# The first loads of a four-layer linear-attention and gated-MLP kernel: two x blocks whole, one on each DMA queue, the first weights split over both queues, twelve idle matmuls

## Chip, cores, metric

One core of a Trainium2 chip. The metric is the device time of one execution in microseconds. The profiler takes one execution; the other times have no profile. A profiled execution's own time is its span plus about 1.8 us, so one can say for each profile whether it was a quick or a slow execution of its kernel.

In the lines of the profile, PE is TensorE's matmuls, PEld its loads of the stationary operand, DVE is VectorE, ACT ScalarE, POOL GpSimd and SP SyncE. An idle matmul multiplies zeros and nobody uses its result; it only keeps TensorE busy until data arrives. "Warm" means that matmuls with 512 columns start 0.216 us apart, "cold" that they start 0.43 us apart, at half the clock.

## The reference

Four layers on x of shape (1, 2048, 1024) in bf16, attention and MLP in turn, each with a layernorm ahead and a residual:

```python
x = x + _A_ref(_layernorm(x), A_wqkv, A_wo)      # linear attention, 32 heads
x = x + _B_ref(_layernorm(x), W_gate, W_up, W_down)   # relu-gated MLP, F = 3584
x = x + _A_ref(_layernorm(x), A_wqkv, A_wo)
x = x + _B_ref(_layernorm(x), W_gate, W_up, W_down)

# in _A_ref:
qkv = (x @ wqkv)...
pq, pk = phi(q), phi(k)
kv = einsum("bhsd,bhse->bhde", pk, v)
```

The change touches only what happens in the first 20 us: layernorm of the first four blocks of 128 tokens (x0 to x3), their transposes, and the first units of k = x @ wqkv. "Unit (j, c)" below is block j times the 512 columns kc, 8 matmuls.

## The kernel before

The loads of the head, in program order. A load without a queue goes out from SyncE (SP); `nc.scalar` sends it from ScalarE (ACT). `k0(0, H)` loads the first half of the first weights (4 of 8 tiles of 128 rows, 512 KB), `k1()` loads 1 MB.

```python
for _ in range(10):
    nc.tensor.matmul(idle, lhsT=zero[:, 0:P], rhs=zero, start=True, stop=True)

k0, k1, v0, q0, q1 = (ring.place() for _ in range(5))
self.load_x(0, 0, nc.scalar)      # columns 0..511 of block 0, 128 KB
self.load_x(0, 1)                 # columns 512..1023
self.load_x(1, None, nc.scalar)   # block 1 whole, 256 KB
k0(0, H)
self.load_x(2, None, nc.scalar)
k0(H, 2 * H)
self.load_x(3, None, nc.scalar)
k1()
q0()
self.load_x(4)
# ... cut: x5 to x7, q1, x8 to x15, v0
```

The work that waits for them. VectorE and ScalarE keep this order (a manual schedule):

```python
def block0():
    stat(0, 0); stat(0, 1)     # VectorE, statistics of both halves of x0
    rstd(0)
    stat(1, 0)                 # VectorE, first half of x1: ahead of the scale of x0
    scale(0, 0); scale(0, 1)
    t0 = turn(0, 0); t1 = turn(0, 1)   # 8 transposes on TensorE
    t0("s")
    stat(1, 1); rstd(1)
    t1("v")
    k(0, 0, between)           # 8 matmuls; "between" puts x1's scale and transposes into it
```

Of the kernel before, what the change touches and what calls it, by code (L numbers as in the profile page):

```python
# [18 lines left out]
class _Ring:  # L19
# [9 lines left out]
    def place(self):  # L29

        name, src = self.plan[self.loaded]
        t = self.pool.tile([P, 8, NW], BF16, tag="w")
        self.tiles[name] = t
        self.loaded += 1
        return lambda lo=0, hi=8: self.nc.sync.dma_start(out=t[:, lo:hi, :], in_=src[:, lo:hi, :])

    def load_to(self, n):
        while self.loaded < min(n, len(self.plan)):
# [40 lines left out]
class _Net:  # L79
# [131 lines left out]
    def head(self):  # L211

        nc, tc, ring = self.nc, self.tc, self.ring
        H = self.KT // 2

        zero = self.ep.tile([P, NW], BF16, tag="e")
        nc.vector.memset(zero, 0.0)
        idle = self.ps3.tile([P, NW], F32, tag="b")
        for _ in range(10):
            nc.tensor.matmul(idle, lhsT=zero[:, 0:P], rhs=zero, start=True, stop=True)  # L220

        k0, k1, v0, q0, q1 = (ring.place() for _ in range(5))
        self.load_x(0, 0, nc.scalar)
        self.load_x(0, 1)
        self.load_x(1, None, nc.scalar)
        k0(0, H)
        self.load_x(2, None, nc.scalar)
        k0(H, 2 * H)
        self.load_x(3, None, nc.scalar)
        k1()  # L230
        q0()
        self.load_x(4)
        self.load_x(5)
        self.load_x(6)
        self.load_x(7)
        q1()
        for t in range(8, self.ST):
            self.load_x(t)
        v0()
        src = self.xb  # L240
        self.xnT[0, 0] = self.xnTp.tile([P, self.KT, QT * P], BF16, tag="xnT", name="xnT0_0")
        stats = [self.small.tile([P, 2, nc.vector.BN_STATS_DIM], F32, tag="stats", name=f"st{j}")
                 for j in range(QT)]
        rs, xn = {}, {}

        def stat(j, c):
            self.ln_stat(j, src[j], c, stats[j])

        def rstd(j):
            rs[j] = self.ln_rstd(stats[j])  # L250
            xn[j] = self.xn_home(0, j)

        def scale(j, h=None):
            self.ln_scale(src[j], *rs[j], xn[j], h)

        def turn(j, h):
            tp = self.ps3.tile([P, H, P], BF16, tag="b")
            for i in range(H):
                kt = h * H + i
                nc.tensor.transpose(tp[:, i, :], xn[j][:, kt * P:(kt + 1) * P], self.ident)  # L260
            dst = self.xnT[0, 0][:, h * H:(h + 1) * H, j * P:(j + 1) * P]

            def take(engine):
                if engine == "v":
                    nc.vector.tensor_copy(out=dst, in_=tp)
                else:
                    nc.scalar.activation(out=dst, in_=tp, func=ACT.Copy)

            return take

        return stat, rstd, scale, turn
# [468 lines left out]
```

## Time and profile before

| | before |
|---|---|
| timed runs beside the change | 1629.17, 1629.21, 1629.38, 1629.8 us |
| the execution that was profiled | 1630.68 us (span 1628.9) |
| TensorE busy | 1621.7 us of 1628.9 |
| x0 complete / second half of k0 / k1 | 3.75 / 10.19 / 13.37 us from the start |
| first transposes / first projection matmul / unit (1,0) | 6.38 / 7.46 / 11.56 us |

The completion times are those of the last of the 16 DMA engines that share a transfer.

### The profile page before, as it was taken

Reading aid. Unit: us, or ns where it says so; the run is one execution under the profiler, and the core shown is the slowest. Engines: PE = TensorE matmul, PEld = TensorE weight load, DVE = VectorE, ACT = ScalarE, POOL = GpSimd, SP = SyncE. Lnnn points to the kernel's source line nnn. Section 1 sums busy time; section 2 is a strip of 40 time slices with the busy share of each in tenths; the row PEclk is TensorE's granted clock in tenths of the full one; section 3 lists DMA queues with packets and bytes.
Section 4 is the critical chain, followed back from the end, with each engine's and each line's share of the span. In section 5 each row is a group of like instructions: output and inputs, shape, how many; then the busy total and the mean of one; then the engine's idle time right before and its main releaser. Section 6 shows DMA issues by size and latency. Waiting matters only on the chain.

```text
span 1628.9 us, 18772 instructions
## 1 busy us (share of the span) xinstructions
PE 1621.7 (100%) x7754; PEld 739.3 (45%) x7754; DVE 566.7 (35%) x940; ACT 331.8 (20%) x638; POOL 201.9 (12%) x134
## 2 busy tenths in 40 slices
PE   8999999999999999999999999999999999999999
PEld 4444444444444444444444444444444444444444
DVE  7845695213212222212165547942022111111211
ACT  5741212101110110111066312121011101101110
POOL 2349220000000000000023592100000000000000
DMA  7312647448445444544560147464554454454452
GB/s 245 65 52 56 178 71 206 144 148 232 155 143 190 160 151 161 168 147 137 168 128 1 53 93 250 85 193 146 182 165 152 155 184 155 145 166 154 155 162 71
DMA packets 298246, 235.06 MB, mean 144 GB/s; under 512 B 101296, under 2 KB 294192, under 8 KB 298160
## 3 DMA queue, kind: packets, MB, share of 16 engines
q1 hardware_dynamic: 292832, 228.75, 47.7%
q10 hardware_dynamic: 5328, 5.11, 0.9%
q8 instruction: 60, 0.98, 0.3%
q14 instruction: 26, 0.21, 0.0%
HBM read 201.33 MB, written 8.39 MB: 129 GB/s over the span
## 4 chain that ended last, share of the span: by engine, by line
PE 98%; ACT 1%; DVE 1%; DMA 1%; issue 0%; SPq 0%; DVEq 0%
PE pu L639 24%; PE pg L639 24%; PE acc L663 23%; PE ps L404 12%; PE ps L530 7%; PE ps L439 7%; DMA t<-in_A_wqkv_dram 1%; PE kv L452 0%; PE acc_last L663 0%; ACT e L351 0%; ACT e L350 0%; PE fold L515 0%; DVE st L138 0%; ACT e L352 0%; DVE slab L358 0%
## 5 line engine op out<-in xcount | busy, mean ns | idle before, releaser
L639 PEld LDWEIGHTS <-t 128*128 128x128 bf16 x3584 | 350.3, 98 | 423.2
L639 PE MATMUL pu<-xnT,t 128*128 128x512 bf16 x1792 | 423.5, 379 | 0.0
L639 PE MATMUL pg<-xnT,t 128*128 128x512 bf16 x1792 | 423.4, 379 | 0.0
L663 PE MATMUL acc<-t,hT 128*128 128x512 bf16 x1764 | 382.5, 379 | 0.0
L645 DVE TENSOR_TENSOR hT<-pu,rg 128x512 bf16<-128x512 f32 x224 | 154.7, 691 | 572.0 <-PE pu L639 572.0
L644 ACT ACTIVATE rg<-pg 128x512 f32<-128x512 f32 x224 | 133.5, 596 | 737.3 <-PE pg L639 737.0
L663 PEld LDWEIGHTS <-hT 128*128 128x128 bf16 x1820 | 177.9, 98 | 209.1
L404 PE MATMUL ps<-t,xnT 128*128 128x512 bf16 x1024 | 224.3, 380 | 2.2 <-DMA t<-in_A_wqkv_dram 1.7
L404 PEld LDWEIGHTS <-xnT 128*128 128x128 bf16 x1024 | 99.2, 98 | 122.3 <-issue 4.3
L530 PE MATMUL ps<-T,pqT 128*128 128x512 bf16 x512 | 111.2, 379 | 0.0
L145 ACT ACTIVATE rstd<-mv,eps 128x1 f32<-128x1 f32 x64 | 18.7, 293 | 334.1 <-DVE mv L143 333.9
L680 DVE TENSOR_TENSOR xo<-x,acc 128x512 bf16<-128x512 f32 x31 | 21.3, 688 | 170.3 <-PE acc L663 170.3
L483 POOL TENSOR_TENSOR prod<-pq,zrow 128x1024 f32<-128x1024 bf16 x32 | 67.9, 2122 | 85.9 <-DVE den L488 72.5
L138 DVE BATCH_NORM_STATS2 stats<-x 128x6 f32<-128x512 f32 (+1 forms) x120 | 78.0, 673 | 0.8
L530 PEld LDWEIGHTS <-pqT 128*128 128x128 bf16 x512 | 49.9, 98 | 60.4 <-issue 0.5
L419 POOL CAST ksum<-x 128x512 f32<-128x512 bf16 x2 | 1.7, 866 | 605.4 <-DVE x L358 605.4
L677 DVE TENSOR_TENSOR x<-x,acc 128x512 f32<-128x512 f32 x32 | 21.6, 675 | 138.5 <-PE acc L663 137.4
L421 POOL TENSOR_TENSOR ksum<-ksum,slab 128x512 f32<-128x512 f32 x46 | 54.0, 1183 | 84.6 <-DVE slab L358 75.1
L358 DVE SCALAR_TENSOR_TENSOR pq<-ps,e 128x512 bf16<-128x512 f32 x64 | 44.0, 688 | 53.9 <-ACT e L352 52.2
L495 POOL TENSOR_TENSOR pq<-pq,den 128x1024 bf16<-128x1024 bf16 x32 | 61.7, 1933 | 3.1 <-DVE den L490 3.1
L488 DVE TENSOR_REDUCE den<-prod 128x32 f32<-128x1024 f32 x32 | 39.0, 1217 | 53.9 <-POOL prod L483 53.9
L439 PE MATMUL ps<-slab,x 128*128 128x512 bf16 x256 | 56.6, 379 | 0.0
(57 smaller groups left out, 596.0 us busy)
## 6 DMA issues: line engine op xcount, KB each, us to landing
t<-in_B_W_gate_dram SPq DMA_DIRECT2D x56, 1024.0 KB, 7.1
t<-in_B_W_up_dram SPq DMA_DIRECT2D x56, 1024.0 KB, 5.4
t<-in_B_W_down_dram SPq DMA_DIRECT2D x64, 896.0 KB, 5.2
t<-in_A_wqkv_dram SPq DMA_DIRECT2D x11, 1024.0 KB, 5.6
t<-in_A_wo_dram SPq DMA_DIRECT2D x4, 1024.0 KB, 7.2
away<-x SPq DMA_DIRECT2D x8, 512.0 KB, 4.4
x<-away SPq DMA_DIRECT2D x8, 512.0 KB, 8.5
out_dram<-xo ACTq DMA_DIRECT2D x31, 128.0 KB, 2.5
```

Of the source, the lines that this page charges most:

```text
L138: self.nc.vector.bn_stats(out=stats[:, c, :], in_=src[:, c * fmax:(c + 1) * fmax])
L358: nc.vector.scalar_tensor_tensor(out=out, in0=ps, scalar=0.0, in1=e, op0=ALU.max, op1=ALU.add)
L404: nc.tensor.matmul(by_row(ps), lhsT=self.xnT[l, l_q][:, kt, j * P:(j + 1) * P], rhs=w[:, kt, :].rearrange("p (b i d) -> p i b d", i=R, d=H ...
L421: nc.gpsimd.tensor_tensor(out=ksum[:, cols], in0=ksum[:, cols], in1=pk, op=ALU.add)
L439: nc.tensor.matmul(ps, lhsT=self.xn[l, t][:, d * P:(d + 1) * P], rhs=self.pk[l, t][:, h * NW:(h + 1) * NW], start=(t == 0), stop=(t == sel ...
L483: nc.gpsimd.tensor_tensor(out=prod, in0=pq_of[sc, j], in1=zrow, op=ALU.mult)
L495: nc.gpsimd.tensor_tensor(out=heads(pq), in0=heads(pq), in1=den[:, :].unsqueeze(2).to_broadcast([P, D // HD, HD]), op=ALU.mult)
L530: nc.tensor.matmul(ps, lhsT=pqT[sc][:, g, j * P:(j + 1) * P], rhs=T[g // 2][:, g % 2, n2 * NW:(n2 + 1) * NW], start=(g == 0), stop=(g == G ...
L639: nc.tensor.matmul(ps, lhsT=w[:, kt, fi * P:(fi + 1) * P], rhs=self.xnT[l, q][:, kt, :], start=(kt == 0), stop=(kt == KT - 1))
L644: nc.scalar.activation(out=rg, in_=pg, func=ACT.Relu)
L645: nc.vector.tensor_tensor(out=h[:, fi, :], in0=pu, in1=rg, op=ALU.mult)
L663: nc.tensor.matmul(ps[:, 0:n], lhsT=hT[ft // 4][:, ft % 4, j * P:(j + 1) * P], rhs=wd[:, k, i * n:(i + 1) * n], start=(ft == 0), stop=(ft ...
```

## The change

The intent, as the diff shows it: have the first two blocks arrive together, bring the second half of k0 sooner by giving half of the first weights to each queue, and let x2 and x3 come later; two more idle matmuls so that TensorE stays warm.

```diff
-        for _ in range(10):
+        for _ in range(12):
...
-        self.load_x(0, 0, nc.scalar)
-        self.load_x(0, 1)
-        self.load_x(1, None, nc.scalar)
+        act = nc.scalar
+        self.load_x(0, None, act)
+        self.load_x(1)
+        k0(H, 2 * H, act)
         k0(0, H)
-        self.load_x(2, None, nc.scalar)
-        k0(H, 2 * H)
-        self.load_x(3, None, nc.scalar)
+        self.load_x(2, None, act)
         k1()
+        self.load_x(3, None, act)
         q0()
```

(The helper that places weights got a `queue` argument; its line is cut. Line numbers of the changed kernel are one higher than before.)

More of the change, by code (lines that the diff above doesn't have):

```diff
@@ L34, in place @@
         self.loaded += 1
-        return lambda lo=0, hi=8: self.nc.sync.dma_start(out=t[:, lo:hi, :], in_=src[:, lo:hi, :])
+        return lambda lo=0, hi=8, queue=None: (queue or self.nc.sync).dma_start(
+            out=t[:, lo:hi, :], in_=src[:, lo:hi, :])
     def load_to(self, n):
```

## The prediction

> **What bounds the kernel now.** I began with the page: how full TensorE is, and what the chain that ended last is made of.
>
> ```profile
> span 1628.9 us, 18772 instructions
> ...
> PE 1621.7 (100%) x7754; PEld 739.3 (45%) x7754; DVE 566.7 (35%) x940; ACT 331.8 (20%) x638; POOL 201.9 (12%) x134
> ...
> PE 98%; ACT 1%; DVE 1%; DMA 1%; issue 0%; SPq 0%; DVEq 0%
> ```
>
> TensorE is idle for 1628.9 - 1621.7 = 7.2 us in the whole span. The diff touches only the loads and idle matmuls of the first microseconds, so no part of it can be worth more than a piece of those 7.2 us (0.4%). Asked from 45 us to the end, the waits of TensorE are an empty list: whatever the start gains or loses is handed to the end one for one. The waits of TensorE in the first 20 us are these (us in total, times, longest):
>
> ```profile
> PE ps L404 <- DMA t<-in_A_wqkv_dram: 1.7, 1, 1.7
> PE idle L220 <- DVE zero L217: 1.3, 1, 1.3
> PE tp L260 <- DVE x L154: 0.6, 1, 0.6
> PE ps L404 <- ACT xnT L267: 0.4, 1, 0.4
> ```
>
> The 1.3 us before the first instruction is not touched. The other waits belong to the change. The timeline of the head says in what order they come (start, duration, engine, line, work, and in brackets the idle time before it and its releaser):
>
> ```profile
> 1.34 4.45 PE L220 MATMUL idle<-zero 128*128 128x512 bf16 x10 [1.34 <-DVE zero L217]
> ...
> 3.78 1.29 DVE L138 BATCH_NORM_STATS2 st<-x 128x6 f32<-128x512 bf16 x2 [2.49 <-DMA x<-in_A_x_dram]
> ...
> 6.38 0.72 PE L260 MATMUL tp<-ident,x 128*128 128x128 bf16 x8 [0.58 <-DVE x L154]
> ...
> 7.46 1.04 PE L404 MATMUL ps<-t,xnT 128*128 128x512 bf16 x4 [0.37 <-ACT xnT L267]
> ...
> 10.23 0.59 PE L404 MATMUL ps<-t,xnT 128*128 128x512 bf16 x2 [1.73 <-DMA t<-in_A_wqkv_dram]
> ...
> 11.56 3.74 PE L404 MATMUL ps<-t,xnT 128*128 128x512 bf16 x16
> ...
> 13.41 1.39 PEld L404 LDWEIGHTS <-xnT 128*128 128x128 bf16 x7 [0.23 <-issue]
> ...
> 19.28 0.45 PEld L260 LDWEIGHTS <-x 128*128 128x128 bf16 x8 [0.57 <-DVE x L154]
> ...
> 19.74 25.48 PE L404 MATMUL ps<-t,xnT 128*128 128x512 bf16 x116
> ```
>
> Four matmuls use the first half of k0, then TensorE stops until 10.23 us for the second half. Two smaller stops follow. The one at 13.41 us is hidden in "x16": sixteen matmuls at the warm pitch would take 15 x 0.216 + 0.38 = 3.62 us, which is what the next such group takes; this group took 3.74 us, so 0.12 us is lost, at the ninth matmul, the first that uses k1. The third, at 19.28 us, is for the scaled fourth block of x: about 0.25 us by the pitch. After 19.74 us there is none.
>
> When do the weights land? The DMA view of narrow windows gives issue to landing of single transfers:
>
> ```profile
> t<-in_A_wqkv_dram SPq DMA_DIRECT2D x1, 512.0 KB, 8.5
> ...
> t<-in_A_wqkv_dram SPq DMA_DIRECT2D x1, 1024.0 KB, 11.2
> ```
>
> The first is the second half of k0, issued at 1.66 us: 1.66 + 8.5 = 10.2 us, the end of the long stop. The second is k1, issued at 2.20 us: 2.20 + 11.2 = 13.4 us, the end of the short one. By the same view the first half of k0 lands at 1.19 + 4.5 = 5.7, x0's halves at 3.5 and 3.8, x1 at 1.19 + 4.0 = 5.2.
>
> **What the Trainium skill says.** "DMA: Bandwidth & Descriptors", section "Issuing engines are not separate DMA queues": transfers started by different engines run on the same 16 DMA engines and interleave. The trace agrees: from 2 to 5 us, with both queues at work, 334 GB/s flow; from 10 to 13.4 us, with almost only SP's queue, 351 GB/s. So a second queue changes who is served first, not how much arrives. The same page, "Queues, rings and completion order": each DMA engine round-robins between the queues that have work. The trace fits that: from 6 to 7 us the two queues take 45% and 51% of the engines' time. "TensorE: Matmul & The Clock Gate", "Part 1: The HAM clock gate": about 3.4 us of sustained work release the full clock, and back-to-back 512-column matmuls are 427 ns apart cold and 216 ns warm. The trace shows both: the idle matmuls come about 0.43 us apart ((4.45 - 0.63) / 9, with 0.63 us for one), the later ones 0.216.
>
> **The change part by part.**
>
> *x0 whole on ACT, x1 whole on SP.* Before, x0 came as two halves of 128 KB side by side. Now 512 KB share the engines before either is complete. At the 385 GB/s that the trace moves from 3 to 4 us, the additional 256 KB take 0.7 us, but before, a part of k0 already rode beside x0's halves, so less is new: counting the bytes moved, 512 KB are through at about 3.7 us, and the landing signal came 0.4 us or so after the data of the small transfers; so 4.1 to 4.2 us instead of 3.75. Cost: +0.4 us on statistics, scale, transposes and the first real matmul, 7.46 to 7.86 us. x1 comes earlier (5.2 to about 4.2), which is of no use: the statistics of x1 start at 5.22 us because VectorE is then free.
>
> *Half of k0 on each queue, directly behind.* Ahead of a complete k0 there are now 0.5 MB of x and 1 MB of k0, instead of also x2, x3 and some of k1. 1.57 MB at 350 GB/s are 4.5 us, from 2.25 to about 6.7, landing at about 7.1 us if all 16 engines keep pace, and up to 2 us later if one lags (the third rival). The matmuls that use the second half are due at 7.86 + 4 x 0.216 = 8.72 us instead of 10.23. From there to the next unit's start the work is the same: 11.56 - 10.23 = 1.33 us. So unit (1,0) starts at about 10.05 instead of 11.56: 1.5 us sooner at this place. That is the 1.9 us by which the fifth matmul was late (10.23 against 7.46 + 4 x 0.216 = 8.32), less the 0.4 us above.
>
> *k1 behind them.* What has to arrive up to the end of k1 is unchanged: four blocks of x, k0 and k1, 3.15 MB, on engines that are already full. So k1 still lands at about 13.4 us if everything else is equal, while TensorE now wants it at 10.05 + 8 x 0.216 = 11.8. TensorE takes its units in order, so most of the 1.5 us can be given back in a new wait in front of k1. At 350 GB/s the 3.15 MB need 9.0 us, to 11.3, with the landing 11.7. The measured 13.4 is therefore not the mean rate alone; the last of the 16 engines came late. If the new order avoids that, k1 costs nothing; if not, it takes nearly all. I put k1's landing at 12.7, between the two: 0.7 us of gain pass it.
>
> *The third stop.* VectorE reaches the second and third norm sooner, by up to 1.5 us, even while TensorE waits for k1, since these depend on x2, x3 and the early copies. So the scale at 19.28 us should no longer be waited for: 0.1 to 0.25 us.
>
> *Two more idle matmuls.* 2 x 0.43 us, ending at 5.79 + 0.86 = 6.65 instead of 5.79 us. The first transposes are now due at 6.38 + 0.4 = 6.78. They fit in the gap: cost 0, and the clock stays released.
>
> Sum: +0.4 for x0, -1.9 for k0's second half, +0.8 given back at k1, -0.2 at the third stop: -0.9 us, less 0.1 for what I cannot see. 1629.4 - 0.8 = 1628.6 us.
>
> **Rivals.**
> 1. *k1 takes the place of k0 in full.* For it: the byte count. Against it: the count alone gives 11.7, not 13.4. It makes 1629.1 to 1629.4.
> 2. *The wait for k0 just vanishes and k1 is in time.* Then 1.5 + 0.2 us are gained: 1627.7. For it: the bytes would fit; against it: the landing of 13.4 in the kernel before.
> 3. *The halves of k0 are themselves caught by a late engine.* The second half of k0 landed at 10.2 although the total rate would have had it sooner; from 5 to 6 us the transfers fell to 302 GB/s. If a DMA engine falls behind by 2 us again, k0 is complete at about 9, unit (1,0) starts near 11, and k1 caps the rest: 1629.0.
> 4. *ACT is held up by issuing.* It now issues a 512 KB transfer between the x blocks. Its four issues took 1.97 us together before; SP's took up to 4.6 us when its queue was full. ACT's first activation is due at 5.7 us; should its last issue block behind SP's, the norm is late by a microsecond or two: 1630 to 1631. ACT queues only 1.25 MB, less than SP had in hand without blocking (2.1 MB), so I give it one chance in ten.
>
> **Range and chances.** Rivals 1 and 3 on one side and 2 on the other span 1627.7 to 1629.4; run to run the kernel varied from 1629.17 to 1629.8, so I add some tenths: 1627.6 to 1630.0. Two per cent would be 32.6 us, more than four times all the idle time of TensorE; within 2% is all but certain.
>
> **What would show it.** In the timeline of after: first statistics near 4.2 us; transposes near 6.8; the first eight projection matmuls with no wait over 0.3 us for k0; unit (1,0) near 10; a wait for k1 between 10 and 13.4 us, of 0 to 1.6 us, 0.9 at my estimate; the run of 116 matmuls starting near 18.9 instead of 19.74. I am wrong if TensorE stops for k0 for over a microsecond, if k1 is no wait at all, if ACT's first activation comes after 6.5 us, or if anything after 45 us changes by more than 0.3 us.

## The result, and the profile after

| | before | after |
|---|---|---|
| median (range) of 4 runs each | 1629.30 (1629.17 to 1629.80) | 1631.86 (1630.82 to 1632.28) |
| profiled execution | 1630.68 | 1632.28 |
| x0 / second half of k0 / k1 complete | 3.75 / 10.19 / 13.37 | 5.23 / 8.95 / 12.57 |
| transposes / first projection / unit (1,0) / run of matmuls without a stop | 6.38 / 7.46 / 11.56 / 19.74 | 7.86 / 8.94 / 12.73 / 20.93 |

The ratio is 1.0014, 95% interval 0.9997 to 1.0032: within 2% without doubt, but above the predicted range (1627.6 to 1630.0). A ratio here is the mean time of one kernel's fast runs over that of the other's of the same rounds, so not quite the ratio of the medians. Over all nine runs of the changed kernel (with e1 below) and 45 of the kernel before, the medians are 1630.84 and 1629.40: about 1.4 us longer instead of a microsecond shorter. The interval of the ratio contains 1; that the change costs time rests on the groups of runs and on the profiles. The profiled execution of the changed kernel is the slowest of its four.

The page of the changed kernel: TensorE is busy for 1623.5 us, 1.8 more than before, and there is a row PEclk that the page of the kernel before has not. Averaged over slices of 41 us it reads 9 everywhere, which looks harmless; the granted clock of the execution is given as 0.999, before as 1.0.

```profile
span 1630.5 us, 18776 instructions
...
PE 1623.5 (100%) x7756; PEld 740.8 (45%) x7756; DVE 566.7 (35%) x940; ACT 331.8 (20%) x638; POOL 202.0 (12%) x134
...
PEclk9999999999999999999999999999999999999999
```

TensorE's waits of the changed kernel (us in total, times, longest). The wait for weights is gone; the wait before the transposes grew from 0.6 to 1.8 us:

```profile
PE tp L261 <- DVE x L155: 1.8, 1, 1.8
PE idle L221 <- DVE zero L218: 1.3, 1, 1.3
PE ps L405 <- ACT xnT L268: 0.4, 1, 0.4
```

The timeline of the changed kernel for the same stretch:

```profile
1.34 4.75 PE L221 MATMUL idle<-zero 128*128 128x512 bf16 x12 [1.34 <-DVE zero L218]
...
5.25 1.29 DVE L139 BATCH_NORM_STATS2 st<-x 128x6 f32<-128x512 bf16 x2 [3.97 <-DMA x<-in_A_x_dram]
...
7.86 0.72 PE L261 MATMUL tp<-ident,x 128*128 128x128 bf16 x8 [1.76 <-DVE x L155]
...
8.94 2.74 PE L405 MATMUL ps<-t,xnT 128*128 128x512 bf16 x6 [0.37 <-ACT xnT L268]
...
12.73 3.62 PE L405 MATMUL ps<-t,xnT 128*128 128x512 bf16 x16
...
20.47 0.45 PEld L261 LDWEIGHTS <-x 128*128 128x128 bf16 x8 [0.57 <-DVE x L155]
```

Three readings. The statistics start at 5.25 us instead of 3.78, and everything up to the first projection matmul is later by the same 1.5 us. Then six matmuls take 2.74 us: (2.74 - 0.63) / 5 = 0.42 us apart, twice the 0.216 of before, and no wait is in them. That is TensorE at half clock, and no list of waits shows it. The view of narrow windows does, in the column of the granted clock (0.50, the third number from the end); in the trace's record the clock is halved from 8.82 to 12.24 us:

```profile
9.00:10.00 1.00, 1.00 (x3) 0.37 (x4) 0.69 (x3) 0.49 (x2) 0.00 (x0) 0.50 1.06 367
```

And the sixteen matmuls from 12.73 us on take 3.62 us, so there is no wait for k1: it landed at 12.57 us, and its unit was due only at 14.46.

A fourth reading stands at the other end of the trace. The last work of VectorE, before (above) and after (below):

```profile
1625.97 0.42 DVE L680 TENSOR_TENSOR xo<-x,acc_last 128x256 bf16<-128x256 f32 x1 [0.34 <-PE acc_last L663]
1627.17 0.42 DVE L681 TENSOR_TENSOR xo<-x,acc_last 128x256 bf16<-128x256 f32 x1 [0.34 <-PE acc_last L664]
```

Up to there the changed kernel is 1.20 us late, but its span is 1.60 us longer (1630.50 against 1628.90). The other 0.40 us come after the last output has landed: from that landing to the end of the span 0.91 us pass before and 1.31 us after, most of the difference being SyncE standing still for 0.37 us (0.06 before) between two of its closing waits, the second for a DMA that had landed 27 us earlier. All six profiles of the changed kernel and of its variants e1, e3, e7, e8 and e15 have this (1.28 to 1.31 us), the other eleven do not (0.84 to 0.99). So it belongs to the program and not to the execution; why, no run shows.

### The profile page after: what moved, and what is told of

Read it like the earlier page. It is cut to its first block, busy times and chain, and to the rows that moved or that the text cites. A ratio compares the mean times of both kernels' runs of the same rounds, so it can differ in the third digit from the quotient of the medians.

```text
span 1630.5 us, 18776 instructions
## 1 busy us (share of the span) xinstructions
PE 1623.5 (100%) x7756; PEld 740.8 (45%) x7756; DVE 566.7 (35%) x940; ACT 331.8 (20%) x638; POOL 202.0 (12%) x134
## 4 chain that ended last, share of the span: by engine, by line
PE 98%; ACT 1%; DVE 1%; DMA 0%; issue 0%; DVEq 0%
PE pu L640 24%; PE pg L640 24%; PE acc L664 23%; PE ps L405 12%; PE ps L531 7%; PE ps L440 7%; PE kv L453 0%; PE acc_last L664 0%; DMA x<-in_A_x_dram 0%; ACT e L352 0%; ACT e L351 0%; DVE st L139 0%; PE fold L516 0%; ACT e L353 0%; DVE slab L359 0%
```

## Experiments

"Before" in the same rounds had nine runs in each set. Pooled, the kernel before has 45 timed runs, 1629.11 to 1630.96 us, in two groups: 26 of them at 1629.44 or less, the other 19 at 1629.78 or more. Its median is 1629.40, its mean 1629.79. Differences of some tenths of a microsecond are therefore told only where the groups of runs do not overlap, or where a profile shows the step.

The theories, as formed after the first comparison: A, the order of the loads makes x0 late in every run; B, one of the 16 DMA engines falls behind by chance, and it was bad luck; C, the longer idle time lets the clock drop, and that is a second cost on top.

### Repeats: the changed kernel (e1) and the kernel before (e2)

No edit.

> The changed kernel once more, nothing edited. Theory A (order): whole blocks of x side by side make x0 land about 1.4 us later, whatever the run; then x0 lands again at 5.0 to 5.4 us and TensorE again idles 1.5 us or more before the first transposes. Theory B (luck of the start): one or some DMA engines stall at the start and it is chance on which transfer it falls; then x0 lands anywhere from 4.1 to 5.4 us. Theory C (clock), which can hold with either: the idle time before the transposes lets the TensorE clock fall to half, seen as matmuls 0.43 us apart after 8.9 us; expected again where the idle time is over 1.5 us. Time 1631 to 1632.3 if A and C.

> The kernel before once more, nothing edited, as the yardstick. A: x0's halves land again at 3.5 to 3.8 us. B: in one of several runs they land a microsecond later. k1's landing tells how steady the late DMA engine is: 13.4 us again if it belongs to the order, 11.7 to 13.4 if it is chance. Ratio to the kernel before 1.000 within 0.0003.

e1: median 1630.18 (1630.02 to 1632.38); in the profile x0 complete at 5.42 us, and the projection matmuls cold again, here from the fourth on. Its median missed the expected 1631 to 1632.3; only the profiled execution is in that range. e2: median 1630.45 (1629.29 to 1630.89); x0's halves at 3.40 and 3.58, k1 at 12.95, between the 11.7 and 13.4 that the expectation called chance. The changed kernel's nine runs of both sets lie between 1630.02 and 1632.38, and its quickest is slower than 30 of the 45 runs of the kernel before. A and C hold so far. e2's ratio is at the edge of 1.000 within 0.0003 (1.0003, with an interval from 0.9990 to 1.0016): the kernel before has two groups of times that I had not known.

### Only the idle matmuls on the kernel before: 12 (e4), 4 (e11)

```diff
-        for _ in range(10):
+        for _ in range(12):      # e4;  range(4) in e11
```

> The kernel before with 12 idle matmuls instead of 10, only this part of the change. They end at about 6.2 to 6.6 us, the transposes are due at 6.38: cost 0 to 0.25 us at the transposes, and none of it later, because the first matmul of the second half of k0 waits for its weights until 10.2 us anyway. Time as before within 0.2 us under every theory; if it is over a microsecond slower, the idle matmuls themselves are the cause.

> The kernel before with 4 idle matmuls instead of 10, loads untouched: the cost of a cold clock alone. C: TensorE idles 3.3 us before the transposes, the first projection matmuls are 0.43 us apart, and the median rises by 0.6 to 1.6 us, to 1630 to 1631. If the clock costs nothing here, as before: 1629.2 to 1629.6.

e4: median 1629.63 (1629.19 to 1630.18), as before. Its profile is worth more than its time: it is a quick execution (1629.19 us), and shows what the kernel before looks like when it is quick. Its timeline:

```profile
6.36 0.72 PE L260 MATMUL tp<-ident,x 128*128 128x128 bf16 x8 [0.18 <-DVE x L154]
7.44 1.04 PE L404 MATMUL ps<-t,xnT 128*128 128x512 bf16 x4 [0.37 <-ACT xnT L267]
8.72 0.59 PE L404 MATMUL ps<-t,xnT 128*128 128x512 bf16 x2 [0.24 <-DMA t<-in_A_wqkv_dram]
```

The stop for the second half of k0, 1.73 us in the profile that I predicted from, is 0.24 us here, with the same loads. The second half of k0 was complete at 8.68 us instead of 10.19. The difference is the last of the 16 DMA engines: k1 landed on the first engine at 11.2 to 11.3 us in both, and on the last 2.04 us after that in the first profile, 0.48 in this one (1.82 in e2, a slow execution of 1630.45 us). So part of B is right, though not of the change: in these three profiles the wait that the change was to remove is long in the two slow executions (1.73 and 1.48 us) and short in the quick one.

e11: median 1631.16 (1630.49 to 1632.07), a little over the expected 1630 to 1631; its five runs overlap with the slowest of before. Its timeline shows the cold clock with the loads untouched, four matmuls (1.89 - 0.63) / 3 = 0.42 us apart:

```profile
6.33 1.03 PE L260 MATMUL tp<-ident,x 128*128 128x128 bf16 x8 [3.10 <-DVE x L154]
7.63 1.89 PE L404 MATMUL ps<-t,xnT 128*128 128x512 bf16 x4 [0.26 <-ACT xnT L267]
```

### The changed kernel with 20 idle matmuls (e3, e15) and with 10 (e7)

```diff
-        for _ in range(12):
+        for _ in range(20):      # e3 and e15;  range(10) in e7
```

> The changed kernel with 20 idle matmuls instead of 12: eight more at 0.216 us once warm fill 1.73 us, up to about 7.8 us, when the transposes of x0 are due. C: the first projection matmuls are 0.216 us apart, the cold stretch is gone, and the kernel is 1.5 to 1.8 us faster than the changed kernel and about 0.5 us faster than the kernel before (k0 and k1 came 0.8 to 1.2 us earlier): 1628.7 to 1629.2 us. If the clock is not the cause (the lateness of x0 alone costs the time): as the changed kernel, 1631 to 1632.

> The changed kernel with 20 idle matmuls once more, for the clock: its x0 landed early (4.54 us) in the first profile, so the cover was hardly tested. C: no run over 1631.5 (nine runs with 12 idle matmuls had four over 1631.6), and in the profile no projection matmuls 0.43 us apart even if x0 lands at 5.2 us or later. If the clock is not the cause of the slow runs, some of these five are over 1631.6 too.

> The changed kernel with 10 idle matmuls as before. They end about 0.4 to 0.8 us sooner, so the idle time before the transposes is 2 us or more. C (clock): the matmuls after it are cold (0.43 us apart) in the profile, and the median is that of the changed kernel or up to 1 us more, 1630.8 to 1632.4. If the clock matters little in the timed runs: as the changed kernel, within its scatter, 1630.2 to 1631.

e3: median 1630.55 (1630.13 to 1631.35); x0 happened to be complete early, at 4.54 us. The clock stayed up, but the time missed the expected 1628.7 to 1629.2: I still reckoned from the slow profile of before. Its run of matmuls without a stop starts at 18.81 us, 0.93 before that profile's and 0.58 after that of e4, and 0.37 us are lost again at the end of the kernel. e15: median 1631.07 (1630.84 to 1631.45), and here x0 was complete at 5.26 us, as late as in the changed kernel's profile (5.23). It is the clean pair. e15's timeline:

```profile
1.34 6.86 PE L221 MATMUL idle<-zero 128*128 128x512 bf16 x20 [1.34 <-DVE zero L218]
8.04 0.61 PE L261 MATMUL tp<-ident,x 128*128 128x128 bf16 x8
9.12 1.47 PE L405 MATMUL ps<-t,xnT 128*128 128x512 bf16 x6 [0.47 <-ACT xnT L268]
```

The transposes start 0.18 us later than in the changed kernel (the idle matmuls run into them), yet the six projection matmuls take 1.47 us instead of 2.74, and unit (1,0) starts at 11.33 instead of 12.73: 1.40 us from the clock, net of that delay (from the first projection matmul to unit (1,0) 2.21 us instead of 3.79, so 1.58). The two profiled executions took 1630.84 and 1632.28 us. In the timed runs the cover takes away the slow end: ten runs with 20 are at most 1631.45 us, while of nine with 12 four are over 1631.6; the means, 1630.92 and 1631.16, are too close for a verdict, since the longer cover also delays the transposes by a little where the clock would have held. e7, with 10: median 1631.96, none of its five runs under 1631.20, and cold matmuls in the profile. C holds.

### Only the two whole blocks on the kernel before (e6); only they undone on the changed kernel (e5)

```diff
 # e6, on the kernel before               # e5, on the changed kernel
-        self.load_x(0, 0, nc.scalar)     -        self.load_x(0, None, act)
-        self.load_x(0, 1)                -        self.load_x(1)
-        self.load_x(1, None, nc.scalar)  +        self.load_x(0, 0, act)
+        self.load_x(0, None, nc.scalar)  +        self.load_x(0, 1)
+        self.load_x(1)                   +        self.load_x(1, None, act)
```

> The kernel before with only its first loads changed: x0 whole on ACT, x1 whole on SP; k0, x2, x3 and the 10 idle matmuls as before. A: x0 lands at 4.5 to 5.4 us, as in the changed kernel, and the median is 0.8 to 2 us over the kernel before (1630.1 to 1631.3), since k0 is on SP alone behind x1. If whole blocks are harmless and the split of k0 costs: 1629.3, as before.

> The changed kernel with x0 again as two halves, one on each queue, and x1 behind it on ACT; k0 stays split over the queues, 12 idle matmuls stay. Theory A (the order: x0 is complete only when 512 KB are through): both halves of x0 land at 3.5 to 3.8 us, the first transposes at 6.4, TensorE idles under 0.4 us before them, no cold stretch; median 1629.0 to 1629.4, at or a little under the kernel before. If the split of k0 over the queues is what costs: 1630.5 or more, with a wait for k0 over 1 us.

e6: median 1631.46 (1631.06 to 1632.20), all five above all nine runs of before in the same rounds (at most 1630.63); x0 complete at 5.52 us, cold matmuls. This one part costs all that the change costs at the start: the run of matmuls without a stop begins at 20.97 us, with the whole change at 20.93. First two lines of e6's timeline, then one of e5's:

```profile
8.14 0.85 PE L259 MATMUL tp<-ident,x 128*128 128x128 bf16 x8 [2.59 <-DVE x L154]
9.23 2.74 PE L403 MATMUL ps<-t,xnT 128*128 128x512 bf16 x6 [0.23 <-ACT xnT L266]
```

```profile
6.80 0.72 PE L262 MATMUL tp<-ident,x 128*128 128x128 bf16 x8 [0.16 <-DVE x L155]
```

e5: median 1629.71 (1629.47 to 1629.93; 1629.0 to 1629.4 was expected), all five below all nine runs of the changed kernel; x0 at 4.16 us (a little late, one engine lagged), no cold matmuls. With the two blocks as before, the split of k0 and the 12 idle matmuls are harmless, but they gain nothing either: the mean is 1629.70, that of e4, which has the 12 idle matmuls and the old loads, 1629.67. That there is no gain has a reason in the profiles: k0 was complete at 9.06 us in e5, and at 8.68 us in e4 with the old loads, so in a quick execution the split brings nothing sooner.

The intended order of e5 was not kept by the scheduler, as the order of its instructions showed afterwards: it put x4 on SP ahead of k1, 256 KB more, and e5's profile has a wait of 0.5 us for k1. That led to e12.

### x3 moved behind k1 (e12, e10), and a fixed order (e14)

e12 is e5 with `self.load_x(3)` for `self.load_x(3, None, act)`. e10 takes x0 and x1 both as column halves on both queues and also moves x3. e14 fixes the order of SP's and ACT's instructions by hand:

```python
with tc.manual_schedule(engines={SP, Activation}):
    self.load_x(0, 0, act); self.load_x(0, 1); self.load_x(1, None, act)
    k0(0, H); k0(H, 2 * H, act); k1()
    self.load_x(2, None, act); self.load_x(3); q0()
```

> The run with x0 in halves (x1 whole behind it on ACT, k0 split, 12 idle matmuls) with one more edit: x3 behind k1 on SP instead of behind x2 on ACT. In that run k1 landed at 12.8 us and TensorE waited 0.5 us for it. If k1 is held up by the bytes ahead of it, 256 KB fewer bring it 0.7 us sooner, the wait for k1 goes and the median falls by about 0.4 us to 1629.2 or less. If k1 is late because of one late DMA engine alone, k1 stays near 12.8 and the median at 1629.5 to 1629.9.

> A try at a version that keeps the change's idea: x0 and x1 both as column halves on both queues, k0 split over the queues, x2 on ACT, k1, then x3 behind k1 on SP; 12 idle matmuls. Expected of A and of the byte count: x0 lands at 3.6 to 3.9, k0 at 7.0 to 8.0, k1 some 0.7 us sooner than in the run with x0 in halves (12.8 there), at 11.5 to 12.2; no wait over 0.5 us in TensorE's list save the first; median 1628.6 to 1629.2. If x3 then comes too late, VectorE waits for it near 13 us and the gain is gone: 1629.4 to 1630.

> x0 in column halves on both queues, x1 behind on ACT, k0 split over the queues, then k1 on SP and x2 on ACT, x3 behind k1 on SP, in exactly this order (in the earlier tries the scheduler had put x4 or x3 ahead of k1). x0 at 3.6 to 3.8 us, k1 complete at 11.3 to 12.0 if no engine lags, no wait for k1; the wait for the second half of k0 stays 0.2 to 0.9 us. Median 1628.9 to 1629.4, with no runs over 1630, which would be a little under the mean of the kernel before (1629.74). If nothing is gained: 1629.5 to 1629.8 as e5 and e12.

e12: the scheduler put x3 ahead of k1, not behind, so its name is wrong; x4 was behind k1 again, which makes it 256 KB less ahead of k1 than e5, the same comparison. k1 was complete at 11.74 us instead of 12.83 (on the first engine 11.35 instead of 11.99). The wait for k1 went; one for k0 of 0.8 us was there instead. Median 1629.75 (1629.61 to 1629.83): no gain, against the expectation. Some of the 1.1 us is the last DMA engine, which came 0.84 us after the first in e5 and 0.39 in e12. e10: x0 at 3.86 us as expected, but k0 only at 8.98 and k1 at 12.40; median 1630.01, two of five runs over 1632. Missed. e14: x0 at 3.69, then a wait of 3.2 us for the second half of k0, and median 1632.33 (1630.97 to 1633.51). Missed by the most. The late half of k0 is in the DMA view of e14, both loads issued within 8 ns of each other at 1.66 us (size, issue to landing):

```profile
t<-in_A_wqkv_dram SPq DMA_DIRECT2D x1, 1024.0 KB, 9.7
t<-in_A_wqkv_dram ACTq DMA_DIRECT2D x1, 512.0 KB, 10.1
```

The 512 KB on ACT, with only two x transfers ahead in its queue, landed after the 1 MB on SP, at 11.8 us. By the packet records ACT's queue moved nothing at all from 5.0 to 5.5 us and 22 KB in the next half microsecond. Equal shares for both queues, as the prediction has them from the skill, would have landed the 512 KB first; from 5 to 6 us they did not hold. Part of it is again the last engine: the fifteenth of 16 had its share of the 512 KB at 10.48 us, the last 1.3 us later. In this run the second queue was no way past a large transfer issued just before on the other. The Trainium skill, "Perfetto Trace Analysis", section "DMA Instruction — HWDGE (DVE, Sync)", says that the block that generates descriptors is locked for one instruction until it has generated all of them. By that section the lock lies within the issuing instruction, and the two issues had ended at 2.16 and 2.19 us, so it does not by itself explain a silence at 5 us. The trace has no record of that block; the cause stays open, only the order of landing is shown.

No version beat the kernel before. e5 and e12 have its mean (1629.70 and 1629.74 against 1629.79) without its slow group; its quick runs stay the quickest.

### Bytes or packets? (e8, e9, e13)

Two whole blocks side by side came late in all six profiles that have them (5.23, 5.42, 4.54, 5.52, 5.38 and 5.26 us), column halves early in the four profiles with the loads of before (3.75, 3.58, 3.69 and 3.70) and in e5, e10, e12 and e14 (4.16, 3.86, 3.72 and 3.69). The windows of 1 to 3 and 3 to 4 us show the difference in the last column, GB/s (the others are busy times, clock and DMA share; the clock reads 1.00 here though the idle matmuls are 0.43 us apart, since the changed kernel's record of the clock begins at 5.41 us and the kernel before has none). Before:

```profile
1.00:3.00 2.00, 1.66 (x4) 0.59 (x5) 0.28 (x3) 1.01 (x1) 0.29 (x1) 1.00 0.44 123
3.00:4.00 1.00, 1.00 (x4) 0.42 (x3) 0.22 (x1) 0.00 (x0) 0.00 (x0) 1.00 1.07 385
```

After:

```profile
1.00:3.00 2.00, 1.66 (x4) 0.58 (x5) 0.28 (x3) 1.01 (x1) 0.29 (x1) 1.00 0.38 89
3.00:4.00 1.00, 1.00 (x4) 0.42 (x3) 0.00 (x0) 0.00 (x0) 0.00 (x0) 1.00 0.97 319
```

So not only is more asked for ahead of x0's completion; less arrives. Column halves make packets of 1 KB, whole rows packets of 2 KB. From the packet records of before and after: up to 3 us a 2 KB packet took 141 ns on average and up to 740, where 84 is usual; a 1 KB packet took 58 ns, where 46 is usual. It is not each packet that is slow: the medians up to 3 us are the usual 84 and 46, and a few long stalls raise the means. Packets of 1 KB have such stalls too (in e5 84 ns on average, up to 1075). Three runs try to tell bytes from packets: e8 has x0 whole on ACT with the first half of k0 beside it (x1 behind x0); e9 halves x0 by rows (64 partitions on each queue, 2 KB packets, 256 KB); e13 is the changed kernel with x0 and x1 each as two column halves on its own queue (1 KB packets, 512 KB).

```diff
 # e13
-        self.load_x(0, None, act)
-        self.load_x(1)
+        for c in range(2):
+            self.load_x(0, c, act)
+            self.load_x(1, c)
```

> x0 whole on ACT with the first half of k0 (not x1) beside it on SP, x1 behind x0 on ACT; the rest in the order of the kernel before, 12 idle matmuls. A in the form of bytes that compete: SP's packets of 1 KB take half of what ACT's of 2 KB take, so x0 is complete after some 384 KB, landing 3.8 to 4.2 us; median 1629.2 to 1629.8. If a whole block of 2 KB rows is slow by itself at the start, x0 lands at 4.5 us or later here too, and the median is 1630 or more.

> The kernel before with x0 halved by rows (64 partitions a queue, whole rows of 2 KB) instead of by columns (128 partitions, 1 KB each); the bytes ahead of x0's completion stay 256 KB. Theory A-bytes: only the bytes that share the start matter, so x0 lands at 3.6 to 3.9 us and the median is as before, 1629.2 to 1629.8. Theory A-packets: the first packets of 2 KB stall at the start (in the changed kernel 40 to 100 KB less had arrived by 3 us), so x0 lands at 4.2 us or later and the median is 0.4 us or more above the kernel before.

> The changed kernel with x0 and x1 each as two column halves, both halves of a block on that block's queue (x0 on ACT, x1 on SP): the same bytes in the same order ahead of x0's and x1's completion, 512 KB, in packets of 1 KB instead of 2 KB. If the bytes are what costs: x0 is complete at 4.9 to 5.5 us as in the changed kernel and the median stays at 1630.2 to 1632. If the slow first packets of 2 KB are: x0 is complete at 4.2 to 4.6 us (at 3.0 us 210 to 265 KB arrived instead of 154 to 200), TensorE idles under 1 us before the transposes, no cold stretch, median 1629.6 to 1630.2.

| | packets at the start | x0 complete | x1 complete | arrived by 3.0 us |
|---|---|---|---|---|
| before | 1 KB | 3.75 | 5.19 | 225 KB |
| e9 | 2 KB, rows halved | 4.10 | 7.52 | 190 KB |
| e13 | 1 KB, 512 KB first | 4.28 | 4.08 | 276 KB |
| e8 | 2 KB beside 1 KB | 4.76 | 7.10 | 162 KB |
| after | 2 KB, 512 KB first | 5.23 | 5.04 | 154 KB |

e13 points to both, in one profile: with the same bytes ahead, x0 is complete at 4.28 us in packets of 1 KB and at 4.54 to 5.52 in packets of 2 KB. Read so, the bytes are worth some 0.6 us (4.28 against 3.58 to 3.75), the packets with the lag of the last engine 0.3 to 1.2 us more. Nearly all of the second part is the lag: the first engine had its share of x0 at 3.88 us in e13 and at 3.90 to 4.22 in the six profiles with whole blocks, the last engine 0.40 us later in e13 and 0.65 to 1.52 us later in the six. With one profile of e13, and a lag that changes from run to run, it is not shown that the size of the packets makes the lag. e8 met its second expectation (4.5 us or later, 1630 or more). e9's 4.10 lies between its two expectations and settles nothing.

In time these runs are no better, for reasons of their own. e8 and e9 (median 1632.88 both) are slow through x1: in the kernel's order VectorE takes the first statistics of x1 ahead of the scale of x0, so a late x1 stops x0's path too. VectorE's waits in e9, up to 12 us, have a second stop in the same row that is a single one before:

```profile
DVE st L138 <- DMA x<-in_A_x_dram: 4.7, 2, 2.9
```

e13 (median 1630.02, 1629.86 to 1632.03) is slow in its profile through k0: after the four small transfers the engines ran half empty, 159 GB/s from 4 to 6 us against 377 from 6 to 8:

```profile
4.00:6.00 2.00, 1.98 (x7) 0.54 (x5) 1.92 (x5) 0.50 (x2) 0.00 (x0) 1.00 0.63 159
6.00:8.00 2.00, 0.72 (x8) 0.55 (x9) 1.68 (x5) 1.09 (x3) 0.00 (x0) 1.00 1.09 377
```

k0 then came at 8.92 and 9.38 us, TensorE waited 1.9 us for it, and went cold. The four small transfers alone are not the cause: e10 has four too, and 340 GB/s from 4 to 6 us. Why single packets stall at the start, and why the engines ran empty in e13, stays open.

## Why the prediction was wrong

**The sum, term by term.** Between the two profiles, up to the start of the run of matmuls without a stop, the prediction's terms measured:

| term | predicted | measured | from |
|---|---|---|---|
| x0 whole beside x1 | +0.4 | +1.48 | transposes 6.38 to 7.86 |
| second half of k0 | -1.9 | -1.9 | no wait; fifth matmul due 4 x 0.216 after the first |
| idle matmuls, clock | 0 | +1.59 | unit (1,0) at 12.73; warm it were 8.94 + 4 x 0.216 + 1.33 = 11.14 |
| k1 | +0.8 | -0.12 | no wait; the old 0.12 gone |
| third stop | -0.2 | 0 | still 0.25 us at 20.48 |
| rest | +0.1 | +0.14 | VectorE at the transposes of x2 |
| sum | -0.8 | +1.19 | 19.74 to 20.93 |
| after the last output has landed | 0 | +0.40 | closing waits of SyncE, 0.91 to 1.31 |

**The steps that failed first.** "Cost: +0.4 us" for x0 is the mis-sized term that pulls the others. I took the rate of the steady stream (385 GB/s from 3 to 4 us) for transfers that make up the first microsecond, and counted bytes; the runs show that less has arrived by 3.0 us with whole blocks (130 to 202 KB in the six profiles, 194 to 276 KB in the nine with column halves) and that the last of 16 engines ends x0 up to 1.5 us after the first. e6 has this part alone and costs as much as the change; e5 undoes it and the loss is gone.

"They fit in the gap: cost 0, and the clock stays released" is the second. It rested on transposes due at 6.78 us. With x0 late they were due at 7.86, the last idle matmul ended at 6.10 (not at 6.65: the clock was released at 5.41 us, and the last three started 0.34 and 0.22 us apart), and from there to the first projection matmul at 8.94 TensorE had only eight transposes. Cold matmuls followed. e15 against the changed kernel, with x0 equally late, makes this 1.58 us from the first projection matmul on, 1.40 net of the later transposes. It is a cost of the cold executions only, among them both profiled ones. The Trainium skill, "TensorE: Matmul & The Clock Gate", "Part 4: PE-mode transpose", says that transposes do not count as busy for the clock in the same way; 2.84 us with transposes alone (after) ended cold and 1.67 us (before) did not, which fits but does not test it: no run differs in the transposes alone.

**The base was a slow execution.** The -1.9 us came true between the two profiles, and is worth little in time: the profile of before was of an execution of 1630.68 us, and in a quick one (e4, 1629.19 us) the stop is 0.24 us. By the times (26 of 45 in the quick group) most executions probably never had the stop that I subtracted; only one quick execution was profiled. The figure to notice it stood beside the profile: the profiled execution was 1.4 us above the median. I subtracted a wait of the one from the time of the other. In e4 the fifth matmul is 0.42 us late instead of 1.9, and k1 is not waited for; with these the sum would have been near zero (-0.1 us) even with my +0.4.

**What was right, and what was luck.** Within 2%, and the difference at 20.93 us (1.19) is still the difference at the last matmul (1.20). It is not all of the difference, though: "handed to the end one for one" fails by the 0.40 us after the last output. Three of the prediction's own signs of being wrong came true: k1 was no wait, ACT's first activation came at 6.82 us (over 6.5), and the time after 45 us changed by more than 0.3 us. The wait for k0 did vanish, in part by luck: k0 was complete at 8.95 us, not 7.1, and TensorE, due for it at 8.72 by the prediction, would have waited 0.2 us had x0 come as predicted. In e10, e12 and e13, with x0 earlier and k0 split, k0 came at 8.98 to 9.38 us and was waited for, 0.8 to 1.9 us. ACT was not held up by issuing (rival 4): its four issues ended at 2.84 us. The rivals were of the right kind but about the wrong transfer: all four concern k0, k1 or ACT, none x0, on which everything else waits. k1 was no wait since TensorE itself came too late; it landed at 12.57 us, near the 12.7 of the prediction. That its landing is set by the bytes ahead of it agrees with e5 and e12 (1.1 us for 256 KB, of which the first engine shows 0.6).

**Open.** Why single packets stall at the start, and whether their size matters; why the end of the changed kernel takes 0.4 us longer; what makes one DMA engine lag, and by how much in which execution; how many of the timed runs of the changed kernel were cold (the profiles say two of two with 12 idle matmuls, none of two with 20, and the times allow four or so of nine).

## What to carry to other kernels

Before subtracting a wait of a microsecond that the profile shows, compare the profiled execution's own time with the timed runs: a single trace can be of the slow kind, and here the DMA wait was what differed. At the start of this kernel the transfer that everything waits for came earliest as two small halves, one on each queue, in front of all else (3.58 to 3.75 us with the loads of before); a larger neighbour beside it cost more than the weights behind it could give back. When work on TensorE moves later, count again how long it has had no ordinary matmuls, because a cold clock appears in no list of waits, only in the pitch of the matmuls and in the granted clock of narrow windows. And compare the ends of the two traces as well as the place that was changed.

## What the Trainium skill lacked or had wrong

- "DMA: Bandwidth & Descriptors", "Bandwidth": its rates are for whole transfers. It has nothing on the rate of the first microsecond of data, where the runs show 154 KB by 3.0 us with packets of 2 KB and 225 KB with 1 KB, and 2 KB packets of 141 ns on average where the median is 84.
- Same page, "Rules for kernel authors": it advises against halving a transfer over two queues, by partitions, because they share the engines. Halved by columns, a 256 KB block was complete at 3.58 to 3.75 us; whole, beside another load, at 4.54 to 5.52, and whole beside half of k0 at 4.76. Halved by partitions it took 4.10. No run loads x0 whole with only its old neighbours beside it, so the runs do not refute the advice; that row has nothing on halving by columns or on one urgent block at the start.
- No page gives a figure for the spread of the 16 engines on such loads: k1's landing on the last engine came 0.4 to 2.5 us after the first in the profiles, much the same for the loads that followed (except in e14), and different from run to run with the same loads (2.04, 1.82, 0.48 us).
- "TensorE: Matmul & The Clock Gate", "Part 1: The HAM clock gate": it gives an idle window of about 3.4 us before the clock drops. Here 2.84 us that held only eight transposes ended cold, and 2.11 us (e10, from 6.40 to 8.51) did not. Where a trace records the clock, it changes at the ends of stretches of 3.41 us, as the page's window has it (5.41, 8.82 and 12.24 us in the changed kernel), but a stretch need not be idle: the clock fell after stretches that held 0.4 to 1.3 us of ordinary matmuls (0.7 us in the changed kernel). It stayed after one with 1.3 us and eight transposes (e10) and fell after one with 1.3 us and none (e8); what share counts as idle the page does not say, and these two rather speak against leaving the transposes out, as Part 4 does.
- "Perfetto Trace Analysis", "DMA Instruction — HWDGE (DVE, Sync)": it tells of the lock on the descriptor generator but not what large loads issued together on two queues do to each other: 512 KB issued 8 ns after 1 MB on the other queue landed 0.4 us after it, at 11.8 us.
